# Odd residues' odd wavenumbers as pairs of 64-row products, and the filter's odd rows loaded between w2's tiles

## The chip, the cores and the metric

The kernel runs on one NeuronCore of one Trainium2 chip. The metric is device time in microseconds (us) of one execution. Three runs of the kernel before took 126.07, 126.17 and 126.58 us; their median is 126.17.

## The reference

Two branches work on sequences of S = 2048 rows, and a gate mixes them.

```python
def _A_ref(x, w_r, w_i):
    X = rfft2(x, axes=(-2, -1)); X = X * (w_r + 1j * w_i)
    return irfft2(X, s=(S, D), axes=(-2, -1))
def _B_ref(x, w1, b1, w2, b2):
    h = layernorm(x)
    u = gelu(einsum("bsd,sf->bdf", h, w1) + b1)
    return (einsum("bdf,fs->bds", u, w2) + b2).transpose(0, 2, 1)
g = sigmoid((x * gate_w).sum(-1)); out = g * a + (1 - g) * b
```

x is 2048 x 512 in bf16, w_r and w_i are 2048 x 257, w1 is 2048 x 1792 and w2 is 1792 x 2048. Branch A is a two-dimensional Fourier transform, a multiplication by a complex filter and the inverse transform; branch B is a layer norm and two dense layers that mix the rows.

## The kernel before, in words

**Dense layers.** The first layer (`m1`, L716) is 14 tiles of F by 16 row tiles j, 224 matmuls of 128x512; its weights sit in one buffer `wa` (tiles 0 to 6) and two buffers `wb` (7 to 10 and 11 to 13). Its results go through a gelu (L732). The second (`m2`, L1065) is again 14 by 16 matmuls. w2's tiles use the same buffers again: tile group 0 can be loaded only when the last L716 on `wa` is over, the last three tiles only when L716 is over altogether. Six PSUM banks (four `acc`, in places two `fb`) hold sums of `m2` that are not finished.

**Transform.** Rows are split by residue r modulo 4. The forward transform along rows is done with table products (L565 to L568) and a radix-4 butterfly on VectorE (`radix4`), then along columns (L664). Wavenumbers along the rows are kept in two halves: `lt` = 0 the even ones, `lt` = 1 the odd ones. `tb2` builds the array B of each half with a few edge columns (L686 to L688). The filter sits in `W` and is multiplied in by two products for each half (`mul`, L839), `comb` and `ob`. Mean and Nyquist columns are treated apart in `c0a`, `c0b`, `c0c`, the Nyquist row in `nyq` on a single partition (L810 to L815); a small path `lines`, `linem` repairs row 0 of B through two small DMAs and a matmul.

The inverse transform along the rows (`i1`, `i1s`) makes, for each half h of the columns and each residue r, a product of B with a table `ti`. For odd residues the even wavenumbers go through `i1s` (L897): the rows are cut in two halves of 64, each half is a product of its own, into a bank of its own (fa, fb), and VectorE adds and subtracts the two (`eo2`, L905). The odd wavenumbers of odd residues go through `i1` with 128 rows and 256 columns (L925), and ScalarE copies the result straight to `zz` (L940). Then `fq`, the inverse transform along the columns (`i3`, L1008 to L1012), the scaling by the gate (L1016), and the sum with branch B (L1071, L1078, L1084).

**Order.** All work is given to a planner as tasks: engine, duration, what is read and written, and a priority. It simulates the engines by its own durations and writes down one order for each engine; that order is fixed in the program, and an engine waits where an input is not there. Lower numbers of `prio` go first: transform products have 0 to 5, `m1` 10, `m2` 20, so dense matmuls fill the places where no transform product is ready. All loads but three are issued by SyncE (SP) in one queue order.

**Filter loads.** `ld_W` (L435) loads one component (real, imaginary) with 16 DMAs: four for `wt` (two of them single rows), whose rows PE turns round with a flip matrix (`wf`, L768, copied by L772 and L780), eight for the odd wavenumbers' rows, three for the even ones (one a single row) and one for the Nyquist row `wn`. `wprep` (L789) needs both components.

## Time and profile before

| what | value |
|---|---|
| median of three runs | 126.17 us |
| profiled execution | 126.11 us |
| its span (first to last instruction) | 124.3 us |
| PE busy | 119.8 us, 96% of the span |
| VectorE (DVE) busy | 113.2 us, 91% |
| ScalarE (ACT) busy | 83.7 us, 67% |
| DMA traffic | 23.10 MB |
| granted PE clock | full in all slices |

Busy time of PE is the union of the matmuls' spans; matmuls are pipelined and their ends are modelled, so the distance from start to start tells what one costs. L numbers are lines of the kernel before. In the order of time, the first column is the start in us from the span's start, the second the time in us, then engine, line, operation, output<-input with shapes, a count, and in brackets the idle time before it and who ended it. In a list of waits the numbers are: us in total, times, longest us.

### The profile page before, as it was taken

Reading aid. Unit: us, or ns where it says so; the run is one execution under the profiler, and the core shown is the slowest. Engines: PE = TensorE matmul, PEld = TensorE weight load, DVE = VectorE, ACT = ScalarE, POOL = GpSimd, SP = SyncE. Lnnn points to the kernel's source line nnn. Section 1 sums busy time; section 2 is a strip of 40 time slices with the busy share of each in tenths; the row PEclk is TensorE's granted clock in tenths of the full one; section 3 lists DMA queues with packets and bytes.
Section 4 is the critical chain, followed back from the end, with each engine's and each line's share of the span. In section 5 each row is a group of like instructions: output and inputs, shape, how many; then the busy total and the mean of one; then the engine's idle time right before and its main releaser. Section 6 shows DMA issues by size and latency. Waiting matters only on the chain.

```text
span 124.3 us, 2226 instructions
## 1 busy us (share of the span) xinstructions
PE 119.8 (96%) x789; PEld 67.7 (54%) x789; DVE 113.2 (91%) x271; ACT 83.7 (67%) x176; POOL 0.2 (0%) x4
## 2 busy tenths in 40 slices
PE   7799999999999999999999999999999999999990
PEld 2245555555645466644445555555577576665590
DVE  1789999999999999999999999999969999999951
ACT  3696889699999999999520003742279999993200
POOL 0000000000000000000000000000000000000000
PEclk9999999999999999999999999999999999999999
DMA  3999999992459946699999930000000000003751
GB/s 112 316 329 306 397 394 385 376 300 62 112 121 258 289 97 121 157 395 406 420 414 415 422 132 0 0 5 0 3 0 0 5 0 0 0 12 131 287 211 42
DMA packets 18203, 23.10 MB, mean 186 GB/s; under 512 B 2174, under 2 KB 15888, under 8 KB 18192
## 3 DMA queue, kind: packets, MB, share of 16 engines
q1 hardware_dynamic: 17616, 22.34, 52.9%
q10 hardware_dynamic: 576, 0.62, 1.6%
q8 instruction: 6, 0.10, 0.3%
q14 instruction: 5, 0.04, 0.1%
HBM read 20.84 MB, written 2.10 MB: 185 GB/s over the span
## 4 chain that ended last, share of the span: by engine, by line
PE 93%; DMA 2%; DVE 1%; ACT 0%; issue 0%
PE acc L1065 33%; PE acc L716 31%; PE fb L716 6%; PE fb L1065 6%; PE fa L716 3%; DMA x<-in_A_x_dram 2%; PE fb L664 1%; PE fa L664 1%; PE fa L565 1%; PE fa L566 1%; PE fa L897 1%; PE fb L1012 1%; PE fa L1012 1%; PE fa L568 1%; PE fa L567 1%; PE fb L925 1%
## 5 line engine op out<-in xcount | busy, mean ns | idle before, releaser
L716 PE MATMUL acc<-h,wb 128*128 128x512 bf16 x112 | 27.0, 379 | 0.0
L1065 PE MATMUL acc<-gl,wb 128*128 128x512 bf16 (+1 forms) x98 | 24.7, 372 | 0.0
L1065 PE MATMUL acc<-gl,wa 128*128 128x512 bf16 (+1 forms) x98 | 24.0, 371 | 0.0
L1071 ACT ACTIVATE x<-acc,ombb,omg 128x512 bf16<-128x512 f32 x12 | 9.0, 780 | 19.3 <-PE acc L1065 19.3
L1065 PEld LDWEIGHTS <-wa 128*128 128x128 bf16 x126 | 13.4, 113 | 9.6
L1065 PEld LDWEIGHTS <-wb 128*128 128x128 bf16 x126 | 13.2, 114 | 9.4
L716 PE MATMUL acc<-h,wa 128*128 128x512 bf16 x64 | 17.1, 379 | 0.0
L716 PEld LDWEIGHTS <-wb 128*128 128x128 bf16 x112 | 10.7, 98 | 10.3
L716 PEld LDWEIGHTS <-wa 128*128 128x128 bf16 x112 | 10.3, 98 | 10.9 <-DMA wa<-in_B_w_dram 1.1
L489 DVE BATCH_NORM_STATS2 stats<-x 128x6 f32<-128x512 bf16 x12 | 8.1, 676 | 2.1 <-DMA x<-in_A_x_dram 2.1
L746 ACT ACTIVATE x<-x 128x512 bf16<-128x512 bf16 x16 | 10.0, 654 | 0.0
L571 ACT CAST xp<-fa 128x512 bf16<-128x512 f32 x16 | 9.0, 594 | 1.5 <-PE fa L568 1.4
L716 PE MATMUL fb<-h,wa 128*128 128x512 bf16 x32 | 9.9, 379 | 0.0
L732 ACT ACTIVATE gl<-acc,b1f 128x512 bf16<-128x512 f32 x11 | 7.8, 711 | 2.8 <-PE acc L716 2.8
L537 ACT ACTIVATE h<-x,nmr,rstd 128x512 bf16<-128x512 bf16 x11 | 8.4, 806 | 1.3 <-DVE nmr L528 1.1
L716 PE MATMUL fa<-h,wa 128*128 128x512 bf16 x16 | 6.1, 378 | 0.9 <-DVE h L531 0.9
L664 PEld LDWEIGHTS <-X 128*128 128x128 bf16 x64 | 4.7, 98 | 2.2
L1016 ACT ACTIVATE B<-fb,g 128x512 bf16<-128x512 f32 x8 | 5.5, 689 | 0.0
L1016 ACT ACTIVATE B<-fa,g 128x512 bf16<-128x512 f32 x8 | 5.5, 685 | 0.0
L671 ACT CAST X<-fb 128x512 bf16<-128x512 f32 x8 | 5.1, 639 | 0.0
L671 ACT CAST X<-fa 128x512 bf16<-128x512 f32 x8 | 5.1, 635 | 0.0
L741 DVE TENSOR_TENSOR x<-x,gw 128x2048 bf16<-128x2048 bf16 x4 | 4.7, 1214 | 0.0
(183 smaller groups left out, 234.8 us busy)
## 6 DMA issues: line engine op xcount, KB each, us to landing
wb<-in_B_w_dram SPq DMA_DIRECT2D x11, 512.0 KB
wa<-in_B_w_dram SPq DMA_DIRECT2D x7, 512.0 KB
wa<-in_B_w_dram SPq DMA_DIRECT2D x2, 896.0 KB
wb<-in_B_w_dram SPq DMA_DIRECT2D x4, 384.0 KB
out_dram<-x SPq DMA_DIRECT2D x3, 512.0 KB
x<-in_A_x_dram SPq DMA_DIRECT2D x2, 512.0 KB
wa<-in_B_w_dram SPq DMA_DIRECT2D x4, 224.0 KB
rot<-dft_ti SPq DMA_DIRECT2D x1, 768.0 KB
```

Source lines behind the costliest of these rows:

```text
L489: V.bn_stats(out=t["stats"][:, j, :], in_=t["x"][:, j // 4, j % 4, :])
L537: add("ACT", 0.71, lambda j=j: A.activation(t["h"][:, j // 4, j % 4, :], t["x"][:, j // 4, j % 4, :], ActF.Identity, bias=t["nmr"][:, j:j ...
L571: add("ACT", act(512), lambda r=r, dq=dq: A.copy(xe(r)[:, :, :, dq, :], t["pa", r, dq][:]), reads=[("pa", r, dq)], writes=[("X", r, dq)], ...
L664: T.matmul(pb[:, k % 2, k // 2], lhsT=t["X"][:, lt, EX[e], c, k, :], rhs=tbl(k, c), start=True, stop=True)
L671: A.copy(t["X"][:, lt, EX[e]].rearrange("p c j l -> p (c j l)").rearrange("p (h c g b) -> p h c g b", h=2, c=2, b=2)[:, :, c], t["pb", lt, ...
L716: T.matmul(t["u", ft][:], lhsT=w[:, j // 4, j % 4, c * P:(c + 1) * P], rhs=t["h"][:, j // 4, j % 4, :], start=(j == jorder[0]), stop=(j == ...
L732: gelus.append(add("ACT", act(512, 1) , lambda ft=ft: A.activation(t["gl"][:, ft, :], t["u", ft][:], ActF.Gelu_apprx_tanh, bias=t["b1f"][: ...
L741: add("DVE", tt(2048), lambda r=r: V.tensor_mul(t["x"][:, :, r, :], t["x"][:, :, r, :], t["gw"][:, None, :].to_broadcast([P, 4, D])), read ...
L746: A.activation(t["x"][:, q, r, :], t["x"][:, q, r, :], ActF.Copy, accum_out=t["glog"][:, 4 * q + r:4 * q + r + 1])
L1016: A.activation(eo_v(p)[:, n].rearrange("p h (n w) -> p h n w", w=2), t["i3", j][:].rearrange("p h (w n) -> p h n w", w=2), ActF.Copy, scal ...
L1065: T.matmul(t["y", j, m][:, cs], lhsT=w[:, o, 512 * q + r:512 * q + 512:4], rhs=t["gl"][:, ft, cs], start=(ft == 0), stop=(ft == NFT - 1))
L1071: A.activation(tbuf(j).rearrange("p h d -> p (h d)"), t["y", j, 0][:], ActF.Identity, bias=t["ombb2"][:, j:j + 1], scale=t["omg"][:, j:j + 1])
```

## The change

The odd wavenumbers of odd residues are now made as the even ones are: `i1s` runs for both halves `lt`, with 64-row products in pairs, one into an fa and one into an fb bank. For this the odd wavenumbers are stored in another order (`sig`, blocks of 16 rows), so that the partners of a pair lie 64 rows apart; the table `ti` shrinks from 3072 to 2112 columns. For `lt` = 1, `eo2` makes the sum, the difference, and from the difference's two parts a sum and a difference again; a factor of the square root of 2 that is left out there goes into the even half's table (`root`) and out again through the gate `g` (`omga`). As before ScalarE copies two banks for each group, now into `zo`.

The loads of the filter follow the new row order. `ld_W` keeps the four large DMAs of even rows; the single rows go into tasks of their own (`single`); the odd rows come in 16 tasks of two DMAs with 64 rows each (`ld_odd`), whose priorities lie between those of w2's tiles. w1's last four loads move between the two components of `ld_W`.

Several small VectorE operations change too: `sp0` and two operations of `sp1` go; the edge columns of `tb2` take fewer operations, and two of them move to ScalarE (`tb2c`); `c0a` and the first part of `omg` move to ScalarE; `c0b` is done once for both halves; `wprep` now waits for the second `bfly`; the Nyquist row is spread over 16 partitions by a DMA (`nspread`), and `nyq` comes after the first half's `ob`; the flips `wf` wait for gelu 7 and 9; `linem` comes after the second `ob`.

```diff
     p = np.arange(P)
-    r4 = np.arange(4)
+    sig = 97 - 32 * (p % 64 // 16) + 2 * (p % 16) - p // 64
...
-    ti = np.zeros((P, 3072))
+    ti = np.zeros((P, 2112))
...
-        th = ang(s, 1 + 4 * (p ^ 96), S)
+        th = ang(s, 1 + 4 * sig, S)
...
+            root = np.where(p < 64, 1.0, 2.0 ** 0.5)
+            v[:, 0:P], v[:, P:256] = np.cos(th), -np.sin(th)
+            v[0, P:256] = alt * (0.5 ** 0.5 if r == 1 else -(0.5 ** 0.5))
+            v[:, 0:P] *= root
+            v[:, P:256] *= root
+            th = ang(1 + 4 * sig, s[0:64], S)
+            v[:, 256:320], v[:, 320:384], v[:, 384:448] = -np.sin(th), np.cos(th), np.sin(th)
...
-        t["wn"] = sb([1, 2, WL], BF16, "wn")
+        t["wn"] = sb([16, 2, 17], BF16, "wn")
+        t["vs"] = sb([16, 2, 16], BF16, "vs")
+        t["na"] = sb([16, 2, 2, 16], F32, "na")
+        t["nn"] = sb([16, 2, 16], BF16, "nn")
         t["ta"] = sb([P, 4, 640], BF16, "rot")
...
-            add("SP", 0.5, ld_wb(k, q), writes=[("w1", k + 1, 4 * q + r) for r in range(4)], prio=10 + 12 * k + 0.1 * q,
+            add("SP", 0.5, ld_wb(k, q), writes=[("w1", k + 1, 4 * q + r) for r in range(4)], prio=(17.1 + q // 2 + 0.2 * (q % 2)) if k else 10 + 0.1 * q,
...
+            dma(t["wn"][:, comp, 0:16], wsrc[comp][1024, 0:256].rearrange("(a b) -> a b", b=16))
...
+        w, u, v, z = rows(comp)
+        dma(u[64:127], v[65:128, :, 0])
+        dma(u[0:64], v[64:128, :, 2])
+        dma(w[1:64, 0, :, 0], v[1:64, :, 0])
+        dma(w[64:P, 0, :, 0], v[0:64, :, 2])
+
+    def ld_odd(comp, n):
+        w, u, v, z = rows(comp)
+        h, o = n % 2, n // 2
+        dma(w[64 * h:64 * h + 64, 1, o, 1], v[:, 3 - o, 3].rearrange("(o i h) l -> h o i l", o=4, h=2)[h][:, ::-1])
+        c, f = 64 * h + 16 * o, 97 - 32 * o - h
+        dma(w[c:c + 16, 1, :, 0], v[f:f + 31:2, :, 1])
 
     for comp in range(2):
-        add("SP", 12.3, ld_W(comp), writes=[("W", comp), ("wt", comp)], prio=17 + 8 * comp, nbytes=300000, after=[a0])
-        if comp == 0:
-            load_wb(1)
+        add("SP", 2.1, lambda comp=comp: ld_W(comp), writes=[("W", comp), ("wt", comp)], prio=17 + comp, nbytes=530000, after=[a0], late=(3.0, 4.0)[comp])
+        for n, at in enumerate((0.2, 0.25, 0.4, 15.8, 15.9)[:5 - comp]):
+            add("SP", 0.6, lambda comp=comp, n=n: single(comp, n), writes=[("Ws", comp, n)], prio=17 + comp + at, nbytes=2000, after=[a0], late=1.0)
+    load_wb(1)
+    for k in range(16):
+        add("SP", 1.0, lambda k=k: ld_odd(k // 8, k % 8), writes=[("Wl", k // 8, k % 8)], prio=31.25 + 0.5 * (k * 7 // 12) + 0.01 * k if k < 12 else 36 + 0.01 * k, nbytes=190000, after=[a0], late=0.5)
...
-    add("DVE", tiny(1), sp0, reads=dk, writes=["sp"], prio=0)
...
-        V.tensor_scalar_mul(sd[:, 0, 0, 1], sd[:, 1, 1, 1], c)
-        V.tensor_scalar_mul(sd[:, 1, 0, 1], sd[:, 0, 1, 1], -c)
-        V.tensor_add(fx[:, 1, 0], sp[:, 0, 1], sd[:, 0, 0, 1])
-        V.tensor_sub(fx[:, 3, 0], sp[:, 0, 1], sd[:, 0, 0, 1])
-        V.tensor_sub(fx[:, 1, 1], sd[:, 1, 0, 1], sp[:, 2, 1])
-        V.tensor_add(fx[:, 3, 1], sd[:, 1, 0, 1], sp[:, 2, 1])
-    add("DVE", tiny(12), sp1, reads=["sp"], writes=["fx"], prio=0)
+        for i, k in ((1, c), (3, -c)):
+            V.scalar_tensor_tensor(fx[:, i, 0], sd[:, 1, 1, 1], k, sp[:, 0, 1], op0=Alu.mult, op1=Alu.add)
+        for i, f in ((1, Alu.subtract), (3, Alu.add)):
+            V.scalar_tensor_tensor(fx[:, i, 1], sd[:, 0, 1, 1], -c, sp[:, 2, 1], op0=Alu.mult, op1=f)
+    add("DVE", tiny(10), sp1, reads=dk, writes=["fx"], prio=0)
...
-                        for i in range(2):
-                            bh, vh = b[:, i::2], v[:, 2 * i:2 * i + 2]
-                            V.tensor_sub(bh[:, :, 1:3, 0], vh[:, :, 0, 0:4:3, 0], vh[:, :, 1, 0:4:3, 0])
-                            V.tensor_copy(bh[:, :, 0:4:3, P], vh[:, :, 0, 1:3, 0])
-                            V.tensor_copy(bh[:, :, 1:3, P], vh[:, :, 1, 1:3, 0])
+                        V.tensor_sub(*tb2e(lt, 1, 0), tb2v(lt)[:, :, :, 1, 0:4:3, 0])
+                        if lt == 0:
+                            for k in (0, 2):
+                                V.tensor_copy(*tb2e(lt, k, P))
...
+    def tb2c():
+        for k in (0, 2):
+            A.copy(*tb2e(1, k, P))
+    add("ACT", 0.45, tb2c, reads=[("R", 1, i, c) for i in range(4) for c in range(2)], writes=[("B", 1, i) for i in range(4)], prio=4.4)
...
-        V.tensor_scalar(t["omg"][:], t["g"][:], -0.5, 0.5, op0=Alu.mult, op1=Alu.add)
-        V.tensor_scalar(t["g"][:], t["g"][:], 0.5, 0.5, op0=Alu.mult, op1=Alu.add)
...
-    add("DVE", 0.4, omg, reads=["b2h"], writes=["g", "omg"], prio=0)
...
+    def omga():
+        A.activation(t["omg"][:], t["g"][:], ActF.Copy, bias=0.5, scale=-0.5)
+        A.activation(t["g"][:], t["g"][:], ActF.Copy, bias=0.5, scale=0.5)
+        A.activation(t["g"][64:P, 1:NJ:2], t["g"][64:P, 1:NJ:2], ActF.Copy, scale=0.5 ** 0.5)
+    add("ACT", 0.6, omga, reads=[], writes=["g", "omg"], prio=4.5)
+    add("DVE", 0.15, omg, reads=["b2h"], writes=["g", "omg"], prio=0)
...
-                add("PE", mm(256, 256), wf, reads=[("wt", comp), "flip"], writes=[("pw", comp, lt, a)], prio=5, alloc=[tag])
+                add("PE", mm(256, 256), wf, reads=[("wt", comp), ("Ws", comp, 0), ("Ws", comp, 1), "flip"], writes=[("pw", comp, lt, a)], prio=5, alloc=[tag], after=[gelus[7 + 2 * comp]])
...
-    add("DVE", 0.4, wprep, reads=[], writes=[("W", 0), ("W", 1), "wpm"] + wtk, prio=1)
+    wpt = add("DVE", 0.2, wprep, reads=[("W", 0), ("W", 1)] + wtk + [("Wl", comp, n) for comp in range(2) for n in range(8)], writes=["wpm"], prio=1)
...
-        def c0a(lt=lt):
-            b, c0 = t["B"][:, lt], t["c0"][:, lt]
...
-        add("DVE", 0.2, c0a, reads=bk, writes=[("c0", lt)], prio=0)
...
+            def c0a():
+                b, c0 = t["B"], t["c0"]
+                A.copy(c0[:, :, :, 0, :], b[:, :, :, 0:2, 0])
+                A.copy(c0[:, :, :, 1, :], b[:, :, :, 3:1:-1, 0])
+            add("ACT", 0.45, c0a, reads=[("B", i, e) for i in range(2) for e in range(4)], writes=[("c0", i) for i in range(2)], prio=4.5)
+        if lt == 0:
+            def nspread():
+                for v in range(2):
+                    dma(t["vs"][:, v], t["B"][0:1, 0, 0, 2 + v, :].rearrange("p (a b) -> p a b", b=16))
+            b0 = [("B", 0, e) for e in range(4)]
+            add("SP", 1.0, nspread, reads=b0, writes=["vs"], prio=34.45, nbytes=1024, late=1.0)
...
             def nyq():
-                pz = sb([1, 1280], F32, "X")
-                na = pz[:, 0:1024].rearrange("p (i v l) -> p i v l", i=2, v=2)
...
-                    V.tensor_mul(na[:, i], v, wn[:, i, None, 0:L].to_broadcast([1, 2, L]))
...
+                V.tensor_mul(na[:], t["vs"][:, None].to_broadcast([16, 2, 2, 16]), wn[:, :, None, 0:16].to_broadcast([16, 2, 2, 16]))
...
-            add("DVE", 3 * d1(512) + 0.35, nyq, reads=[("B", i, e) for i in range(2) for e in range(4)] + [("W", 0), ("W", 1), ("c0", 0)] + pbk, writes=["nn"], prio=0.5)
...
-        def c0b(lt=lt):
...
+            nyt = add("DVE", tiny(6), nyq, reads=["vs", ("Ws", 0, 3), ("Ws", 0, 4), ("Ws", 1, 3), ("c0", 0)], writes=["nn"], prio=3.25)
...
+        def c0b():
...
+            V.tensor_mul(cm[:, 0], c0[:, :, :, 0], pm[:, 0])
...
+        if lt == 0:
+            add("DVE", tiny(6), c0b, reads=[("c0", 0), ("c0", 1), "wpm"], writes=[("ce", 0), ("ce", 1)], prio=3.22)
...
-        add("DVE", 2 * tt(2048), bfly, reads=bk, writes=["xs"], prio=pr)
+        bt = add("DVE", 2 * tt(2048), bfly, reads=bk, writes=["xs"], prio=pr)
+        if lt:
+            wpt.deps.add(bt)
...
-            add("DVE", tt(4096), mul, reads=["xs", ("W", comp), ("W~", comp, lt)], writes=[("pp", "st")[comp]], prio=pr)
+            add("DVE", tt(4096), mul, reads=["xs"] + ([("Wl", comp, n) for n in range(8)] if lt else [("W", comp), ("W~", comp, 0)] + [("Ws", comp, n) for n in range(3)]), writes=[("pp", "st")[comp]], prio=pr)
...
+        obt = add("DVE", tt(2048) + 2 * tt(1024), ob, reads=["xs"], writes=bk, prio=pr)
+        if lt == 0:
+            nyt.deps.add(obt)
...
-                dma(t["s9"][8:9], t["nn"].rearrange("p v l -> p (v l)"))
+                for v in range(2):
+                    dma(t["s9"][8:9, L * v:L * v + L].rearrange("p (a b) -> p a b", b=16), t["nn"][:, v])
...
-    add("PE", mm(512), linem, reads=["s9", "tb"], writes=["pl8"], prio=3, alloc=["fa"], after=[combt])
+    add("PE", mm(512), linem, reads=["s9", "tb"], writes=["pl8"], prio=3, alloc=["fa"], after=[obt])
...
-        if rs:
-            def i1s(h=h):
...
+        for lt in range(2 * rs):
+            def i1s(h=h, lt=lt):
...
+                p2 = t["i1s", h, lt] = [ps([P, 2, 2, P], F32, tag, 2) for tag in ("fa", "fb")]
...
+                            f = (320 - 64 * c) if lt else c * P
...
-                                T.matmul(p2[m][:, n, v], lhsT=t["B"][k, 0, r, 2 * c + v, h:L:2], rhs=ti[k, 2 * c * P:2 * c * P + P], start=(c == 0), stop=(c == 1))
-            i1t[h, 1, 0] = i1t[h, 3, 0] = add("PE", MMR, i1s, reads=[("T", 0, 1), "ti"], writes=[("i1s", h)], prio=3, alloc=["fa", "fb"])
+                                T.matmul(p2[m][:, n, v], lhsT=t["B"][k, lt, r, 2 * c + v, h:L:2], rhs=ti[k, f:f + P], start=(c == 0), stop=(c == 1))
...
+            def eo2(h=h, lt=lt):
+                e, o = (t["zo"][:, lt, h, m ^ lt] for m in range(2))
+                if lt == 0:
+                    for k, f in enumerate((V.tensor_add, V.tensor_sub)):
+                        f(t["zz"][:, 1, h, 0, :, k].rearrange("p v r a -> p r v a"), e, o)
+                    return
+                zv = t["zz"][:, 1, h, 1].rearrange("p v k r a -> p r (v k) a")
+                x = lambda u: u.rearrange("p r v (k a) -> p r (v k) a", k=2)
+                V.tensor_add(zv[:, :, :, 0:64], x(e), x(o))
+                V.tensor_sub(e, e, o)
+                V.tensor_sub(zv[:, :, 0:4:2, 64:P], x(e)[:, :, 0:4:2], x(e)[:, :, 1:4:2])
+                V.tensor_add(zv[:, :, 1:4:2, 64:P], x(e)[:, :, 0:4:2], x(e)[:, :, 1:4:2])
+            add("DVE", 2 * tt(512) + 2 * tt(256) * lt, eo2, reads=[("zo", h, lt, m) for m in range(2)], writes=[("zz", h, r, lt) for r in (1, 3)], prio=3.55)
...
-            for lt in range(rs, 2):
-                tag = ("fa", "fb")[lt if not rs else r // 2]
+            for lt in range(0 if rs else 2):
+                tag = ("fa", "fb")[lt]
...
-                        if r % 2:
-                            for c in range(2):
-                                f = (5 - c) * P
-                                T.matmul(p1[:, v], lhsT=d(c), rhs=ti[:, f:f + L], start=(c == 0), stop=(c == 1))
...
-                        V.tensor_copy(k0[:, :, :, 0], e[:, :, :, 0])
-                        V.tensor_copy(k1[:, :, :, 0], e[:, :, :, P])
+                        V.tensor_copy(t["zz"][:, 0, h, :, :, :, 0, 0].rearrange("p i v k -> p (i v) k"), e[:, :, :, 0:P + 1:P].rearrange("p i v k -> p (i v) k"))
```

More of the change, by code (lines that the diff above doesn't have):

```diff
@@ L460, in ld_ti @@
     def ld_ti():
-        t["ti"] = sb([P, 3072], BF16, "rot")
+        t["ti"] = sb([P, 2112], BF16, "rot")
         dma(t["ti"][:], tabs["ti"])
@@ L948 @@
+                add("ACT", act(512), i1ev, reads=[("i1", h, r, lt)] + pbk, writes=[("ze", h, r, lt)], prio=1.7, free=[tag], after=[lined])
             if r % 2 == 0:
```

153 lines of the change are left out of this document (64 added, 89 removed).

## The prediction

> **What bounds the kernel now.** I read the page first, sections 1, 2 and 4: TensorE (PE) is busy in every slice but the first two and the last, and the chain that ended last is nearly all matmul.
>
> ```profile
> span 124.3 us, 2226 instructions
> ...
> PE 119.8 (96%) x789; PEld 67.7 (54%) x789; DVE 113.2 (91%) x271; ACT 83.7 (67%) x176; POOL 0.2 (0%) x4
> ...
> PE   7799999999999999999999999999999999999990
> ...
> DVE  1789999999999999999999999999969999999951
> ...
> PE 93%; DMA 2%; DVE 1%; ACT 0%; issue 0%
> ```
>
> Busy need not mean useful, so the waits come next, PE's alone and then the list of all engines.
>
> ```profile
> PE fa L716 <- DVE h L531: 0.9, 1, 0.9
> PE fa L361 <- PEq L1117: 0.8, 1, 0.8
> ```
>
> Both lie before 5.3 us. From there to 121.5 us PE waits for nobody: wherever the transform is not ready, matmuls of the two dense layers (L716, L1065) stand in the order. So a part of PE's work that becomes shorter shortens the end by as much, as long as nobody keeps PE waiting.
>
> VectorE (DVE) is nearly as full, so I looked at the end of its order of time for slack.
>
> ```profile
> 117.49 0.68 DVE L1084 TENSOR_TENSOR x<-x,B 128x1024 bf16<-128x1024 bf16 x1
> 118.41 0.75 DVE L1078 SCALAR_TENSOR_TENSOR x<-acc,omg,x 128x512 bf16<-128x512 f32 x1 [0.23 <-PE acc L1065]
> 119.94 0.48 DVE L1078 SCALAR_TENSOR_TENSOR x<-acc,omg,x 128x256 bf16<-128x256 f32 x1 [0.78 <-PE acc L1065]
> 120.72 0.35 DVE L1078 SCALAR_TENSOR_TENSOR x<-fa,omg,x 128x128 bf16<-128x128 f32 x1 [0.30 <-PE fa L1065]
> 121.50 0.35 DVE L1078 SCALAR_TENSOR_TENSOR x<-fb,omg,x 128x128 bf16<-128x128 f32 x1 [0.43 <-PE fb L1065]
> ```
>
> It waits for PE 0.23 + 0.78 + 0.30 + 0.43 = 1.74 us here: DVE may come about 1.7 us later before the last store moves.
>
> **PE: the products that are replaced.** The old and the new form both stand in PE's order of time, for the old L925 is what goes and the old L897 is what the new ones copy.
>
> ```profile
> 93.73 0.60 PE L925 MATMUL fa<-rot,B 128*128 128x256 bf16 x4
> 94.17 0.22 PE L933 MATMUL fb<-rot,B 128*128 128x128 bf16 x1
> ...
> 96.14 0.59 PE L1065 MATMUL acc<-gl,wb 128*128 128x512 bf16 x2
> 96.66 0.23 PE L897 MATMUL fa<-rot,B 64*128 64x128 bf16 x1
> 96.67 0.23 PE L897 MATMUL fb<-rot,B 64*128 64x128 bf16 x1
> ...
> 97.22 0.62 PE L1065 MATMUL acc<-gl,wb 128*128 128x512 bf16 x2
> 97.77 0.23 PE L897 MATMUL fa<-rot,B 64*128 64x128 bf16 x1
> ...
> 98.33 0.84 PE L1065 MATMUL acc<-gl,wb 128*128 128x512 bf16 x3
> ```
>
> Ends are modelled, so I count from start to start. Four L925 take 94.17 - 93.73 = 0.44 us; there are 16, so 1.75 us go. A group of 16 L897 (8 pairs, the two halves of a pair 0.01 us apart) lies between dense matmuls, which step 0.216 us: the two that start at 96.14 would be over at 96.57, the next starts at 97.22, so the group costs 0.65; the second, from 97.65 to 98.33, 0.68. Of that 8 x 0.055 = 0.44 are the pairs; the remaining 0.22 is paid on going from 128-row to 64-row products and back. Two such groups come in: 1.33 us. Gain 1.75 - 1.33 = 0.42 us. The bounds: nothing if the new groups cost double (no row shows that), and 1.75 - 2 x 0.44 = 0.87 if each new group lies directly beside an old one, so that the change of form is shared. I take 0.42, because a group needs one fa and one fb bank at once, and the copies out of them (ScalarE, ACT, L900) come 0.48 us apart, 0.98 to 1.1 us per group:
>
> ```profile
> 97.32 0.60 ACT L900 CAST h<-fa 128x512 bf16<-128x512 f32 x1
> 97.80 0.61 ACT L900 CAST h<-fb 128x512 bf16<-128x512 f32 x1
> 98.43 0.58 ACT L900 CAST h<-fa 128x512 bf16<-128x512 f32 x1
> ```
>
> So two dense matmuls (0.43 us) fit between groups, as now. The Trainium skill, TensorEngine Tiling (Array Packing), says under Theoretical Speedup that a contraction of at most 64 rows gains up to twofold, and under Key Properties that a change of tiling mode drains the engine; by the first the gain would be 0.87, by the second less, and this trace shows the second with its 0.22 us.
>
> **DVE: what goes.** From start to start: L621 and two of L634 to L639, 0.42; the twelve edge operations of L686 to L688 become four, eight at 0.07, 0.57; L800 and L801 twice, to ACT, 0.29; the one-row Nyquist line L810 to L815, from 58.36 to 60.79, 2.43; L820 to L825 twice, 1.01; L789 and L790 0.20; two of L752 to L754 0.27. Before the first filter multiply (L839, 61.15 us) 5.19 us leave. Some of it comes back later: the Nyquist line on 16 rows (six tiny ones, 0.08 each, 0.5), L820 to L825 once (0.5), L789 and L790 (0.2). So DVE stands 4.0 us earlier at the inverse transform. There the paired form asks for more: in place of a plain copy by ACT, eo2 for the odd wavenumbers adds, per half, two 512-element operations (L905 steps 0.34 to 0.37) and two of 256 elements; the nearest rows are L1038 with 129 (0.22) and L955 with 508 (0.34), and I take 0.20 to 0.34, low end. That is 1.08 per half, 2.16 in all, at most 2.7. Two L953 copies become one in each half, -0.15. Net 5.19 - 1.20 + 0.15 - 2.16: DVE ends its own work 2.0 us earlier (1.4 at the high end). It is not the bound, so this is worth nothing by itself; it is cover.
>
> **ACT.** Seven tiny operations arrive (edges, c0, g); the nearest row, L1025 with 128x8, steps 0.11, so 0.8 us. ACT is full from 30 to 57 us and then waits 12.3 us for L1065, in which they are hidden. Copies out of PSUM stay at 16. Cover gone, they would delay copies by 0.8 us.
>
> **SP and the DMAs.** The filter comes in 32 DMAs now (24.44 to 50.47 us, w1's last four between), and w2's first tile is issued at 50.70, though its buffer is free at 35, when L716 turns from wa to wb. After: 8 large, 9 small, 32 of 64 rows, and three more for the Nyquist line, 20 more. A filter DMA takes SP 0.43 (at 33.04) to 0.67 (at 34.61), so +9 to 13 us of issuing. The even rows and w1 should be out by 36 to 43 us, w2's seven tiles (now 3.33 us) and 24 odd pieces (10 to 16, nearer 11, since most of the odd pieces now take 0.43 to 0.52) by 51 to 57, the rest by 62. Waiting behind them are w2's tiles 7 to 10, now issued at 54.14. First use is at 63.7, and with tiles 0 to 6 alone six banks give 42 dense matmuls, 9 us, so PE is covered to 72.8. The last three tiles wait for PE at 63.75 in both kernels. The odd rows are read by DVE at about 67.5. Cost 0; cover about 5 us for DVE. The added waits: filter flips L768 stand behind a gelu, queued before the dense matmuls; the last ACT copies of them end at 55.2 now, DVE would come to the multiply at 56.0. The one-row DMA to 16 rows stands on SP ahead of w2's tile 7, which waits for its buffer then anyhow.
>
> **The sum.** The profiled execution took 126.11 us, its span 124.3 with 1.8 around it, 0.06 below the median 126.17. 126.11 - 0.42 = 125.69, say 125.7. Start and tail (5.3 us and 2.9 us) are untouched.
>
> **Rivals.**
> (A) As forecast, gain 0.2 to 0.6: 125.5 to 125.9. 55%.
> (B) Groups side by side: 0.62 with one such pair, 0.87 with two, 125.2 to 125.5. For it: DVE is 4 us earlier, so all inputs are there when the odd part begins; against it: the two banks. 16%. The twofold gain of the Trainium skill, TensorEngine Tiling (Array Packing), Theoretical Speedup, would lead here.
> (C) The gain is eaten: groups meet more 128-row products between them, or PE's order, which is fixed beforehand from planned times, has small waits: 126.0 to 126.6. For it: every task's planned time changes. Against it: the present order, from the same planner, has no wait. 13%.
> (D) Slower: the filter's rows become the bound. If DVE's 5.19 us are lost at the multiply (flips or odd rows late), DVE ends 1.20 - 0.15 + 2.16 = 3.2 us later than now; 1.74 - 0.42 = 1.3 of that is hidden, so 1.9 us come on top of 125.69: 127.6. It decides from about 3.7 us of waiting at the filter multiplies. Against it: the flips' copies end at 55.2 already now. 9%.
> (E) Slower: PE itself stands before a transform product or a w2 tile, because real landings fall behind the planned ones; 1 us gives 126.7, 2 us 127.7. 7%.
>
> **Numbers.** 0.5% is about what a measurement of this kernel can tell from no change, 0.63 us: faster is below 125.54, slower above 126.80. Faster: B and a tenth of A, 0.22. Slower: D, E and a fifth of C, 0.19. Same: the rest, 0.59. The range that leaves out no more than 2 in 10 is 125.2 to 126.9. A's own is 125.5 to 125.9.
>
> **What would show it.** The 128x256 products at L925 are gone and 64 matmuls of 64x128 stand there, pairs 0.055 us apart; dense matmuls lie between the groups and start 0.65 to 0.68 us apart around each. PE still waits for nothing after 5.3 us. DVE's first filter multiply starts at 56 and its waits for PE at the end grow to more than 3 us. w2's first tile is issued between 36 and 43 us. I am wrong if PE has a wait over 0.3 us on DVE, ACT or a DMA, or if the new groups cost more than 0.87 us each.

## The result and the profile after

The changed kernel takes 132.76 us (median of six runs, 131.60 to 134.51), against 126.12 us of the kernel before in the same runs. The ratio is 1.0507, with a 95% interval from 1.0456 to 1.0557: slower by 5%. The forecast was 125.7 us, between 125.2 and 126.9. The profiled execution took 132.86 us. Below, a median counts all runs of a kernel, while a ratio leaves out those more than 1.5% above the kernel's fastest, so the two can differ.

From the page of the changed kernel: span, busy time, the slices of PE and of its clock, and the chain by engine.

```profile
span 131.1 us, 2256 instructions
...
PE 121.6 (93%) x791; PEld 66.9 (51%) x805; DVE 112.1 (86%) x253; ACT 85.7 (65%) x183; POOL 0.2 (0%) x4
...
PE   7799999999999999999916999999999999999991
...
PEclk9999999999999999999995599999999999999999
...
PE 68%; DVE 10%; DMA 8%; ACT 8%; SPq 2%; issue 2%; DVEq 0%
```

One place stands out: PE is busy for a tenth of the 21st slice (65.6 to 68.8 us) and for six tenths of the 22nd, and its clock is half in the 22nd and 23rd. The chain, 93% PE before, has only 68% PE now and runs in parts through DMAs and SP's queue (SPq). The list of waits (us in total, times, longest us) names w2's tiles and the filter's imaginary rows:

```profile
PEld L1102 <- DMA wb<-in_B_w_dram: 5.8, 4, 2.8
DVE wpm L813 <- DMA W<-in_A_w_i_dram: 4.3, 1, 4.3
PE acc L1102 <- DMA wb<-in_B_w_dram: 4.1, 3, 2.5
```

L1102 is the second dense layer (L1065 before), L813 the part of `wprep` that reads the filter's imaginary component. PE's order of time around the empty slices:

```profile
63.74 1.67 PE L1102 MATMUL acc<-gl,wa 128*128 128x512 bf16 x7
65.25 0.38 PE L1102 MATMUL acc<-gl,wb 128*128 128x512 bf16 x1
66.51 0.41 PE L1102 MATMUL acc<-gl,wb 128*128 128x512 bf16 x1 [0.88 <-DMA wb<-in_B_w_dram]
69.39 0.62 PE L1102 MATMUL acc<-gl,wb 128*128 128x512 bf16 x1 [2.48 <-DMA wb<-in_B_w_dram]
69.80 0.63 PE L1102 MATMUL acc<-gl,wa 128*128 128x512 bf16 x1
71.15 0.62 PE L1102 MATMUL acc<-gl,wb 128*128 128x512 bf16 x1 [0.72 <-DMA wb<-in_B_w_dram]
71.56 2.77 PE L1102 MATMUL acc<-gl,wa 128*128 128x512 bf16 x6
```

After only seven matmuls on w2's tiles 0 to 6 (`wa`), the order asks for tile 7 (`wb`, at 65.25), which landed at 65.17, and then for tiles 8, 9 and 10, which land at 66.46, 69.35 and 71.11. A dense matmul at full clock steps 0.216 us. From start to start the three waits are 1.26 - 0.22 = 1.04, 2.89 - 0.22 = 2.67 and 1.35 - 0.43 = 0.92 us, together 4.63. From 69.39 on the matmuls step 0.427 us (six from 71.56 take 74.12 - 71.56 = 2.56 us), that is at half clock, until 75.1; against 0.216 this costs 2.35 us more. 4.63 + 2.35 = 6.98; less the 0.38 us that the products gain (below) it is 6.60, and PE's last matmul ends 6.80 us later than before (128.26 against 121.46). The other 0.2 us is not assigned; part of it is the start, where the first dense matmul stands 0.05 us later.

SP's order of time shows when the tiles went out:

```profile
40.03 0.37 SPq L307 DMA_DIRECT2D wa<-in_B_w_dram  x1
40.46 2.48 SPq L307 DMA_DIRECT2D W<-in_A_w_r_dram  x4
...
56.13 2.54 SPq L307 DMA_DIRECT2D W<-in_A_w_i_dram  x4
58.72 0.45 SPq L307 DMA_DIRECT2D wa<-in_B_w_dram  x1
59.22 1.04 SPq L307 DMA_DIRECT2D W<-in_A_w_i_dram  x2
60.37 1.26 SPq L307 DMA_DIRECT2D vs<-B  x2
61.72 1.95 SPq L307 DMA_DIRECT2D wb<-in_B_w_dram  x4
63.72 7.72 SPq L307 DMA_DIRECT2D W<-in_A_w_i_dram  x8
...
72.49 1.32 SPq L307 DMA_DIRECT2D wb<-in_B_w_dram  x3
```

A task of two odd-row DMAs keeps SP for 1.04 to 1.27 us, so between two of w2's first seven tiles lie 2.6 to 4.5 us; tile 6 goes out at 58.72 and tiles 7 to 10 from 61.72, 7.6 us later than before (54.14). The last three tiles stand behind the last eight odd-row DMAs and go out at 72.49, 8.7 us later than before. Up to 61 us SP's issuing sets this pace, and not the transfers; this is seen in the busy times by stretch (columns: stretch, its length, busy PE, PEld, DVE, ACT and POOL with their instructions, granted clock, DMA engines' share, GB/s). The kernel before:

```profile
56.00:61.00 5.00, 5.00 (x25) 2.29 (x24) 4.86 (x33) 4.88 (x15) 0.00 (x0) 1.00 1.02 410
```

The changed kernel in the same stretch:

```profile
56.00:61.00 5.00, 4.95 (x24) 2.29 (x24) 4.96 (x5) 4.75 (x17) 0.00 (x0) 1.00 0.66 202
```

Before, seven w2 tiles were queued at once and the DMA engines were full at 410 GB/s. After, they are busy for two thirds and move half as much, while SP is issuing in all but about 0.9 us of the five. Behind 64 us this turns round: from 65 to 69 us the engines are full (share 0.98, 347 GB/s; the row stands in the last section), and tiles 9 and 10 take 6.6 and 7.9 us from issue to landing, where tile 7 took 3.45.

What was to be gained did come in its place. The new pairs, in PE's order of time:

```profile
97.03 0.81 PE L1102 MATMUL acc<-gl,wa 128*128 128x512 bf16 x3
97.77 0.23 PE L939 MATMUL fa<-rot,B 64*128 64x128 bf16 x1
97.78 0.23 PE L939 MATMUL fb<-rot,B 64*128 64x128 bf16 x1
...
98.33 0.84 PE L1102 MATMUL acc<-gl,wa 128*128 128x512 bf16 x3
```

A group lies between 97.03 + 3 x 0.216 = 97.68 and 98.33, 0.65 us, the lower end of what was predicted. DVE's first filter multiply (L868) starts where it was expected, and the second half waits:

```profile
56.16 2.28 DVE L868 TENSOR_TENSOR xp<-xp,W 128x4096 bf16<-128x4096 bf16 x1
...
73.01 0.19 DVE L813 TENSOR_TENSOR wpm<-W 128x16 f32<-128x16 bf16 x1 [4.30 <-DMA W<-in_A_w_i_dram]
...
125.20 0.75 DVE L1115 SCALAR_TENSOR_TENSOR x<-acc,omg,x 128x512 bf16<-128x512 f32 x1 [1.26 <-PE acc L1102]
```

At the end DVE still waits 1.26 + 0.78 + 0.30 + 0.43 = 2.8 us for PE, so its 4.3 us of waiting are hidden behind PE's own loss.

### The profile page after: what moved, and what is told of

Same layout as the page of the kernel before. It is cut to its first block, busy times and chain, and to the rows that moved or that the text cites. A ratio compares the mean times of both kernels' runs of the same rounds, so it can differ in the third digit from the quotient of the medians.

```text
span 131.1 us, 2256 instructions
## 1 busy us (share of the span) xinstructions
PE 121.6 (93%) x791; PEld 66.9 (51%) x805; DVE 112.1 (86%) x253; ACT 85.7 (65%) x183; POOL 0.2 (0%) x4
## 4 chain that ended last, share of the span: by engine, by line
PE 68%; DVE 10%; DMA 8%; ACT 8%; SPq 2%; issue 2%; DVEq 0%
PE acc L1102 31%; PE acc L735 13%; DMA wb<-in_B_w_dram 6%; PE fb L735 5%; PE fb L1102 5%; ACT X L677 3%; PE fa L735 3%; ACT x L765 3%; DMA x<-in_A_x_dram 2%; SPq L307 2%; DVE st L868 2%; DVE xp L868 2%; PE fa L939 2%; DVE B L695 2%; PE fa L576 1%
## 5 line engine op out<-in xcount | busy, mean ns | idle before, releaser
L1102 PE MATMUL acc<-gl,wb 128*128 128x512 bf16 (+1 forms) x94 | 25.0, 383 | 4.5 <-DMA wb<-in_B_w_dram 4.1
L735 PE MATMUL acc<-h,wb 128*128 128x512 bf16 x108 | 26.3, 379 | 0.1
L1102 PE MATMUL acc<-gl,wa 128*128 128x512 bf16 (+1 forms) x96 | 25.1, 390 | 0.1
L1102 PEld LDWEIGHTS <-wb 128*128 128x128 bf16 x126 | 13.3, 115 | 15.4 <-DMA wb<-in_B_w_dram 5.8
L1102 PEld LDWEIGHTS <-wa 128*128 128x128 bf16 x126 | 13.5, 115 | 10.6 <-issue 1.4
L735 PE MATMUL acc<-h,wa 128*128 128x512 bf16 x62 | 16.6, 379 | 0.1
L735 PEld LDWEIGHTS <-wa 128*128 128x128 bf16 x112 | 10.3, 98 | 10.9 <-DMA wa<-in_B_w_dram 1.5
L1121 DVE TENSOR_TENSOR x<-x,B 128x1024 bf16<-128x1024 bf16 x7 | 4.8, 683 | 0.0
```

What stands on the lines that cost most here:

```text
L735: T.matmul(t["u", ft][:], lhsT=w[:, j // 4, j % 4, c * P:(c + 1) * P], rhs=t["h"][:, j // 4, j % 4, :], start=(j == jorder[0]), stop=(j == ...
L1102: T.matmul(t["y", j, m][:, cs], lhsT=w[:, o, 512 * q + r:512 * q + 512:4], rhs=t["gl"][:, ft, cs], start=(ft == 0), stop=(ft == NFT - 1))
L1121: V.tensor_add(o, o, eo_v(p))
```

## The experiments

**Theory 1:** the loads cost all of it. SP's queue cannot issue 32 small DMAs among w2's tiles in the time that the planner assumes, so PE's order, written for planned landings, stands before tiles that have not landed. The plan itself says that tiles 7 to 10 have landed at 61.4, 62.8, 64.1 and 65.5 us; tiles 8 to 10 really landed 3.7, 5.3 and 5.7 us later. Not all of this begins between w2's tiles: tile 7 goes out 6.75 us later than planned, and the first w2 tile already goes out 4.7 us late (40.03, planned 35.31), ahead of the first odd-row DMA. **Theory 2:** the transfers are too slow whoever issues them. **Theory 3:** the new products, edges or DVE's order cost something too.

**The odd rows issued by GpSimd.** The 32 DMAs leave SP's queue.

```diff
-        dma(w[c:c + 16, 1, :, 0], v[f:f + 31:2, :, 1])
...
+        dma(w[c:c + 16, 1, :, 0], v[f:f + 31:2, :, 1], nc.gpsimd)
...
+        add("POOL", 1.0, lambda k=k: ld_odd(k // 8, k % 8), writes=[("Wl", k // 8, k % 8)], prio=31.25 + 0.5 * (k * 7 // 12) + 0.01 * k if k < 12 else 36 + 0.01 * k, nbytes=190000, after=[a0], late=0.5)
```

> The changed kernel with one edit: the 32 DMAs of the filter's odd rows are issued by GpSimd's queue instead of SyncE's; w2's tiles stay on SyncE. Theory 1 (SyncE's queue: the odd pieces take 0.45 to 1 us each of its time, so w2's tiles 7 to 10 are issued at 61.7 and 11 to 13 at 72.5, PE waits 4.6 us and then runs at half clock, 2.4 us more): w2's last three tiles are issued at about 63.8, PE waits for no tile, 125.5 to 126.0. Theory 2 (the packets of 514 bytes between the tiles slow the tiles in the DMA engines, whoever issues them): PE still waits over 2 us for w2, 129 or more. Theory 3 (the 64-row products or VectorE's chain cost the time): 132 as now.

131.86 us, ratio 1.041 (1.034 to 1.048). The waits behind 57 us were gone, but a new loss took their place. GpSimd, which had nothing else to do, began at 1.27 us, while x and w1 were being loaded. Busy times in the same stretch, first of the kernel before:

```profile
5.00:30.00 25.00, 24.71 (x140) 12.84 (x141) 23.45 (x71) 20.81 (x45) 0.00 (x0) 1.00 0.99 334
```

Then of this run:

```profile
5.00:30.00 25.00, 20.94 (x120) 10.54 (x120) 20.60 (x61) 18.28 (x40) 14.92 (x26) 1.00 1.09 275
```

PE lost 3.8 us there; the DMA engines were full in both, but moved 275 GB/s instead of 334. So this run took away one loss and added another, and could not tell the theories apart.

**The even rows issued by GpSimd,** with the same edit on `ld_W` and `single`.

> The changed kernel with one edit: the filter's even rows and single rows (8 large and 9 small DMAs) go to GpSimd's queue; the odd pieces still alternate with w2's tiles on SyncE. Theory 1: SyncE begins the alternating part some 8 to 10 us earlier (40.0 now), so all is issued in time: PE waits less than 1 us, 125.5 to 127. Theory 2: the alternation with small packets is unchanged, so the tiles stay slow; they only begin earlier, PE still waits for the tiles issued after 61 us, 128 or more. Theory 3: 132.

139.63 us, ratio 1.096 (1.087 to 1.106). The same start, worse: PE was busy for 16.69 us of that stretch, and, with the odd pieces still on SP, PE waited for tiles at 74.5 to 78.4 us all the same.

**The loads alone, on the kernel before.** Its products, edges and tables stay; the filter is loaded with the change's tasks, priorities and 64-row pieces (in the old row order).

```diff
+        dma(w[64 * h:64 * h + 64, 1, o, 1], v[:, 3 - o, 3].rearrange("(o i) l -> o i l", o=4)[2 * h:2 * h + 2, ::-1])
+        c, f = 32 * o + 16 * h, 96 - 32 * o + 16 * h
+        dma(w[c:c + 16, 1, :, 0], v[f:f + 16, :, 1])
```

> The kernel before with the changed kernel's loads alone: odd rows in 32 DMAs of 64 rows between w2's tiles, same priorities, the filter preparation after the second butterfly as there; PE's products, the row order and the small VectorE operations are those of before. Theory 1 and 2 (the loads are the cause): PE waits 3 to 6 us for w2's tiles between 64 and 76 us and its clock falls, 131 to 134. Theory 3 (products or VectorE): 126 to 126.6.

The profiled execution took 328 us, and the other three 131.18 to 134.88 us, which gives no ratio. In this profile the clock is not on record, and its matmuls of 512 columns step 0.48 or 0.62 us, so the half clock that the next expectation speaks of is not shown.

> The same kernel as the one before with split loads, for a profile: three of its four executions took 131 to 135 us, and the profiled one 328 with PE at half clock throughout. Theory 1: 131 to 135, PE waits 3 to 6 us for w2's tiles between 64 and 76 us. Otherwise the loads alone don't explain it: 126 to 127.

134.82 us, ratio 1.064 (1.058 to 1.071). Its list of waits has the loss of the changed kernel:

```profile
PEld L1079 <- DMA wb<-in_B_w_dram: 5.8, 6, 2.5
PE acc L1079 <- DMA wb<-in_B_w_dram: 4.0, 3, 2.1
...
PE fa L780 <- DMA wt<-in_A_w_i_dram: 1.6, 1, 1.6
```

So the loads, without any of the new products, are enough for the whole 5%. That it is more comes in part from the last row: here the flips (L780) wait 1.6 us for their even rows, which they don't in the changed kernel. Theory 3 isn't needed for the loss.

**The same DMAs, other numbers for the planner.** Only what the planner believes of a task of odd rows is changed, so the fixed orders come out differently; what is transferred and by whom stays. PE's order changes most, SP's a little (here `ti`'s table goes out behind the last three tiles). Three versions; the first:

```diff
-        add("SP", 1.0, lambda k=k: ld_odd(k // 8, k % 8), writes=[("Wl", k // 8, k % 8)], prio=31.25 + 0.5 * (k * 7 // 12) + 0.01 * k if k < 12 else 36 + 0.01 * k, nbytes=190000, after=[a0], late=0.5)
+        add("SP", 1.3, lambda k=k: ld_odd(k // 8, k % 8), writes=[("Wl", k // 8, k % 8)], prio=31.25 + 0.5 * (k * 7 // 12) + 0.01 * k if k < 12 else 36 + 0.01 * k, nbytes=450000, after=[a0], late=2.5)
```

> The changed kernel with one edit in the planner's numbers: a task of two odd pieces counts 1.3 us of SyncE (1.0 before), 450 kB (190 kB) and lands 2.5 us late (0.5). The DMAs and their priorities stay. Theory 1a (the tiles are late, but what hurts is that PE's order was written for earlier landings: it has tile 7's product second in line when other products are possible): PE's waits shrink to under 1.5 us, 126 to 128.5. Theory 1b (the tiles are so late that no order helps): 131 to 133.

127.77 us, ratio 1.0106 (1.0071 to 1.0141), with 126.53 us before: over 5 of the 6.6 us are back. PE has no wait behind 5.9 us and full clock until 123.9, though tiles 7 to 10 go out from 60.09, only 1.6 us earlier than in the changed kernel, and the last three at 69.39. Now the plan is too late: transform products stand further back than they need to, and DVE waits for them. From the list of waits:

```profile
DVE X L991 <- ACT h L983: 5.2, 1, 5.2
```

The nearer numbers (1.3 us, 380000 bytes, 0.5 us):

> As the run with true durations, but less pessimistic: an odd task counts 1.3 us, 380 kB and lands 0.5 us late, so that the plan's last odd rows (69.2 to 70.5 us) and w2's last tile (76.3) lie nearer to what the trace of that run shows (issued until 69.3 and at 70.7), and the inverse transform's first product is planned at 86.3 and not at 90.4. There the plan was 4 us too late for VectorE, which stood 5.2 us before the inverse transform and then ended last. Theory 1a (the loss is the distance between the planned and the real landings, on either side): PE waits under 0.7 us, VectorE's wait before the inverse transform falls to 1 to 2 us, 125.5 to 126.5. Rival (the loads, late as they are, cost over 1 us under any order): 127 to 129.

127.0 us (125.86 to 128.9, twelve runs; before, 126.24), ratio 1.0024 (0.9992 to 1.0056). In the profiled execution (127.94 us) PE stood some 1.65 us before w2's tiles between 65 and 71 us, and DVE waited 1.9 us, in the old places. From the list of waits:

```profile
PEld L1102 <- DMA wb<-in_B_w_dram: 2.9, 4, 1.2
...
DVE wpm L813 <- DMA W<-in_A_w_i_dram: 1.9, 1, 1.9
```

Expected were 125.5 to 126.5 us and waits of PE under 0.7. The runs of this version lie 3 us apart. It may be that each execution's landings show in its time where the order leaves no room; only one was profiled, so this is not shown. Between the two versions (410000 bytes, 1.5 us):

> Only the planner's numbers for a task of odd rows: 1.3 us, 410000 bytes, 1.5 us late, between the two versions that gave 127.77 (planned too late, PE idle at the end) and 127.0 (planned a little early, PE waits 1.65 us at 65 to 71). Theory 1 (the distance between planned and real landings is the loss): PE's waits for w2 at 65 to 71 fall under 0.8 us while DVE's wait for ACT in the inverse transform stays under 2 us; 126.0 to 126.7. Rival (any order pays, since the transfers themselves are too slow): what PE gains at 65 to 71 is lost at DVE, 127.0 to 127.7.

127.18 us, ratio 1.0047 (1.0014 to 1.0081), with PE's waits for w2 at 1.6 us in the profiled execution, counted as before. It was neither better than the nearer numbers nor as free of waits as the later ones; the sizes that theory 1 gave here did not come out. With all 32 DMAs on SP, none of the three sets of numbers left both PE and DVE free of these waits in the profiled execution. By the ratio the nearer numbers may cost nothing (its interval includes 1); by the medians they cost 0.6%.

**Half as many odd-row DMAs.** The loads alone on the kernel before, alternating as in the change, but 16 DMAs with 128 rows.

> The kernel before with the loads split and alternating as in the run before, but each odd DMA with 128 rows, as the kernel before has them: 16 in place of 32. Alternation and priorities stay, the number is halved, the planner counts 0.5 us for each. Theory 1 (it is SyncE's time for 32 pieces): SyncE is through 6 to 8 us earlier, w2's last tiles go out at 64 to 66 us, PE waits under 1 us, 126 to 127.5. Rival (the alternation itself, whatever the number): PE waits 3 us or more, 130 or more.

128.01 us, ratio 1.0103 (1.0047 to 1.0158). The list of PE's waits in its profile:

```profile
PE fa L781 <- DMA wt<-in_A_w_i_dram: 1.9, 1, 1.9
PE fa L729 <- DVE h L544: 0.9, 1, 0.9
```

No wait for w2 is left: tiles 7 to 10 went out from 57.24 and landed at 62.0 to 66.3, 3.2 to 3.5 us earlier than with 32 DMAs in the run before (65.5 to 69.4). The wait alone would not show it, because PE comes to w2 3.7 us later here: it stands at 38 us, where the flips (L781) wait for their even rows (in the change they stand behind a gelu), and its clock is half from 41.0 to 44.5. A PE 3.7 us earlier would have waited about 0.4 us for tile 10, by an estimate from these landings. So 16 DMAs that alternate make the tiles less late than 32 do, and most of PE's wait goes with them. The expected 126 to 127.5 us, with the last tiles out by 64 to 66, were missed: they went out at 67.60.

**The odd rows on GpSimd, not at the start.** A copy on GpSimd that reads `b2h` stands ahead of them.

> The odd rows on GpSimd's queue again, but its first DMA stands behind a copy of two elements of b2h, which lands at about 26 to 30 us. In the run without that hold GpSimd began at 1.3 us and took DMA time from x and w1 (PE waited 4 to 5 us before 30 us), while after 57 us PE waited for nothing. Theory 1 (SyncE's queue is what made w2 late): PE waits for nothing over 0.3 us after 5.3 us, w2's last tiles are issued at about 64 us, 125.4 to 126.0. Theory 2 (odd packets slow w2's or w1's tiles wherever they are issued): PE waits for a tile between 30 and 75 us, 127 or more.

129.15 us (126.55 to 133.59, twelve runs), ratio 1.0098 (1.0049 to 1.0148). `b2h` landed only at 34 us, so 32 DMAs ran into w2's loads. The profile is of the execution with 133.59 us. SP issued tiles 7 to 10 from 56.94 on, and yet PE had to wait for them until 67.6 to 70.5; here too the plan had them 4.3 to 5.1 us earlier than they landed. Its busy times by stretch:

```profile
56.00:61.00 5.00, 5.00 (x25) 2.25 (x24) 4.97 (x5) 4.75 (x18) 2.13 (x5) 1.00 1.07 261
61.00:65.00 4.00, 4.00 (x21) 1.86 (x19) 4.00 (x6) 2.49 (x8) 1.90 (x4) 1.00 1.03 305
```

Here the DMA engines are full (share 1.07, 1.03) and move 261 to 305 GB/s instead of 410. In the run with the odd rows on GpSimd from the start it was 275 instead of 334. So theory 2 holds in this form: while GpSimd issues small pieces, the full engines move less of the large tiles. For the changed kernel it does not explain why the tiles go out late, as its engines stood at 0.66 there; but from 65 to 69 us, when tiles 8 to 10 are under way, they are full as well, and what part of those landings this makes no run separates.

**Only some of the pieces on GpSimd,** with the nearer numbers: the last four pieces, or the last eight, behind a GpSimd copy that reads a gelu's result.

```diff
+        nc.gpsimd.tensor_copy(t["pj"][:], t["gl"][0:1, 9, 0:2])
+    add("POOL", 0.3, hold, reads=[("gl", 9)], writes=["pj"], prio=0)
+    for k in range(12, 16):
+        add("POOL", 1.2, lambda k=k: ld_odd(k // 8, k % 8, nc.gpsimd), writes=[("Wl", k // 8, k % 8)], prio=1 + 0.01 * k, nbytes=190000, after=[pl.last_w["pj"]], late=1.5)
```

> The changed kernel with the nearer durations (1.3 us and 380000 bytes for a task of odd rows), and the last four pieces (8 DMAs of the imaginary component) issued by GpSimd behind a copy that waits for the tenth gelu, so at about 54 us, instead of by SP before w2's last three tiles. Theory 1 (SP's queue is what holds w2 back): SP is rid of the 7 us that those 8 take behind tiles 7 to 10, the last three tiles go out at 64 to 66 instead of 71.8, PE waits under 0.5 us at 65 to 71, and the time is 125.7 to 126.2. Theory 2 (the 16 DMA engines are the limit, whoever issues): the landings of tiles 7 to 10 do not come earlier, PE waits 1.5 us or more as with nearer durations alone, 126.8 to 127.5.

126.37 us (126.17 to 127.08, twelve runs), ratio 1.0005 (0.9987 to 1.0024); expected were 125.7 to 126.2. SP's order of time in its profile:

```profile
63.05 1.95 SPq L307 DMA_DIRECT2D wb<-in_B_w_dram  x4
65.04 0.46 SPq L307 DMA_DIRECT2D rot<-dft_ti  x1
65.60 1.93 SPq L307 DMA_DIRECT2D wb<-in_B_w_dram  x3
```

And the list of PE's waits, which is complete:

```profile
PE fa L358 <- PEq L1161: 0.8, 1, 0.8
PE fa L735 <- DVE h L542: 0.4, 1, 0.4
```

PE's order of time where it comes to w2:

```profile
63.72 4.05 PE L1109 MATMUL acc<-gl,wa 128*128 128x512 bf16 x18
67.61 0.59 PE L1109 MATMUL acc<-gl,wb 128*128 128x512 bf16 x2
```

Tiles 7 to 10 go out even later than in the changed kernel (61.72) and land later (66.67 to 71.44), and PE waits for none of them: by the plan of this version tile 7 lands at 67.1 us, so the order has 18 matmuls on tiles 0 to 6 first. Two things changed at once here. The planner's numbers move this order; the four pieces on GpSimd do not make tiles 7 to 10 land earlier than with the nearer numbers alone (66.07 to 71.35), but they take away most of the 7 us of SP ahead of the last three tiles (out at 65.60, not 71.79), and DVE's wait of 1.9 us is gone. The whole 5% is back with the same products and the same odd rows.

> As the run with four pieces on GpSimd, but eight, all of the imaginary component (16 DMAs), behind the ninth gelu, so from about 49 us. Theory 1: tiles 7 to 10 go out at 54 to 57 as in the kernel before, PE has no wait behind 5.9 us, 125.6 to 126.0. Theory 2: w2's tiles 3 to 8 share the DMA engines with GpSimd's pieces and land late though issued early; PE waits 1 to 4 us at 60 to 71, 126.8 to 130.

126.44 us, ratio 1.0013 (0.9994 to 1.0031). No wait for a tile either. Tiles 7 to 10 went out from 59.90, not at 54 to 57 (by the plan 57.7 was the earliest), and GpSimd began at 44.38, not at 49; the expected time of 125.6 to 126.0 was not reached.

**Everything but the loads.** The changed kernel's products, DVE and ACT work and table, with the loads of the kernel before. It leaves out the new row order of the odd rows.

> All of the change but its loads: products, DVE, ACT and table ti are the changed kernel's; the filter comes in with the DMAs and in the places of the kernel before (16 for a component, all before w2's first tile; only the Nyquist row goes to 16 partitions). So the odd rows stand in the old order and the output is wrong in the odd wavenumbers; the amounts of work are the changed kernel's. Theory 1 (the loads cost everything, the products are worth what their distances say): PE has no wait after 5.9 us and the time is 126.1 - 0.42 = 125.7, with 125.4 to 125.9. Rival (part of the loss sits in products, edges or the order of DVE, and has been hidden behind the loads): 126.5 or more, with waits of PE on DVE or ACT behind 60 us.

126.01 us (125.91 to 127.05, twelve runs) against 126.2, ratio 0.9993 (0.997 to 1.0016); expected were 125.4 to 125.9. The list of PE's waits has nothing behind 5.5 us:

```profile
PE fa L358 <- PEq L1158: 0.8, 1, 0.8
PE fa L739 <- DVE h L546: 0.2, 1, 0.2
```

Summed from start to start, the 48 old products of the odd residues (L925 and L897) took 1.75 + 1.11 = 2.85 us before; here the 64 pairs' halves take 2.22. The dense matmuls of 512 columns took 45.56 us and now take 45.81, which is the switch into two more groups. Net gain 0.38 us. The last matmul ends at 121.37 instead of 121.46, only 0.09 us earlier: the start and the first layer took 0.28 us more (the first dense matmul stands at 5.42 instead of 5.29, as x's first rows were there 0.14 us later, and there is one wait of 0.14 us at 22.6). Theory 3 falls: without the new loads, the change costs nothing that these runs can tell, and its gain is too small to be told from no change. Tiles 7 to 10 land at 65.96 to 69.82 here, later than with the kernel before, and PE waits for none, as the plan has them at 65.5 to 69.6.

## Why the prediction was wrong

**The step that failed** is "SP and the DMAs", with its result "Cost 0". Its single parts:

- The first w2 tile "between 36 and 43": 40.03, right. "w2's seven tiles and 24 odd pieces by 51 to 57": 60.3. The rate per DMA was right: 24 odd ones kept SP for 11.9 us ("nearer 11") and w2's seven tiles for 3.8 (3.3). What stood nowhere are 1.1 us for three DMAs of the Nyquist row and 3.4 us in which SP issued nothing, together 20.2 us from 40.03 on. The last eight odd pieces took 7.72 us: 4.3 of issuing and 3.4 of waiting. In this trace SP's DMAs take eight semaphores in turn, and none goes out before the one eight places ahead of it has landed: the last two odd pieces go out at 69.36 and 71.12, as tiles 9 and 10 land (69.35, 71.11). SP's waits in the changed kernel:

```profile
SPq L307 <- DMA wa<-in_B_w_dram: 5.4, 6, 1.7
...
SPq L307 <- DMA wb<-in_B_w_dram: 4.0, 5, 1.9
```

- "The rest by 62": the last odd piece was out by 71.4, and with it "the last three tiles wait for PE at 63.75 in both kernels". In the changed kernel they wait for SP until 72.49. This cost PE nothing more here, as PE was late by then.
- "PE is covered to 72.8 by 42 dense matmuls of tiles 0 to 6". This is the error that cost the time. Six banks and seven tiles would allow 42; the order that PE follows has seven of them, and then asks for tile 7. I worked out what PE could do, not what its fixed order does. The run with the last four pieces on GpSimd uses that freedom: 18 matmuls on `wa` before the first on `wb`, and no wait, with landings that are later than the changed kernel's.
- "Cover about 5 us" for the odd rows at DVE: DVE needed them at 68.7 and had them at 73.0. That would have been rival D, hidden here behind PE.

The landings of tiles 7 to 10 side by side (planned: by the kernel's own planner; waits: PE's for these tiles, from start to start):

| kernel | go out from | planned to land | landed | first matmul on tile 7 | PE waits |
|---|---|---|---|---|---|
| before | 54.14 | 65.5 to 69.6 | 64.48 to 68.17 | 65.93 | none |
| changed | 61.72 | 61.4 to 65.5 | 65.17 to 71.11 | 65.25 | 4.63 us |
| nearer numbers | 62.65 | 64.7 to 68.8 | 66.07 to 71.35 | 66.11 | 1.65 us |
| later numbers (first version) | 60.09 | 66.0 to 70.0 | 63.56 to 68.96 | 66.96 | none |
| last four on GpSimd | 63.05 | 67.1 to 71.2 | 66.67 to 71.44 | 67.61 | none |
| products alone | 57.34 | 65.5 to 69.6 | 65.96 to 69.82 | 66.22 | none |

The tiles went out 7.6 to 6.4 us later than before, but landed only 0.7 to 2.9 us later: before, tile 7 stood behind the first seven tiles and took 10.3 us from issue to landing, here 3.45. What moved more is the plan, 4.1 us earlier than before, so that PE's order asked for tiles 8 to 10 before they were there.

**Rival E is what happened:** PE stands before a w2 tile because real landings fall behind the planned ones. It was named with 7% and priced at 126.7 for 1 us and 127.7 for 2 us. Two sizes were missing from it: the wait was 4.6 us, and a further 2.35 us came from the half clock behind it, a term that stood nowhere. With its own rule (125.7 plus the wait) 4.6 us give 130.3, and 132.7 with the half clock, which is the measured time.

**Right were the other steps.** The new groups cost 0.65 us each; the gain on PE is 0.38 where 0.42 was written, though only 0.19 of it is seen between the medians, and the interval includes no gain. Rival B did not occur: there is a dense matmul or more between any two groups. DVE's first multiply started at 56.16 (56.0 predicted). In the run with the products alone DVE ends its own work at 117.07 instead of 118.17, 1.1 us earlier instead of 1.4 to 2.0, of which 0.47 us is a wait for the Nyquist row's DMA that the account had not got. ACT's 0.8 us did not reach PE: with the products alone it has no wait on ACT. The prediction's own test, "I am wrong if PE has a wait over 0.3 us on a DMA", pointed to the right place.

## What to carry to other kernels

Where an engine's order is fixed from planned times, compare these planned landings with real ones before counting on work that could fill a wait; the same transfers cost 6.6 us with one plan and 0.8 to 1.2 us with others. When many small DMAs are put into one queue among large ones, add up that queue's issue times piece by piece to the issue of each large tile, with its waits for DMAs that are still under way; then ask whether the tile lands later too, since here a tile that went out 7.6 us later landed 0.7 us later. And a wait of a few microseconds on PE can have a second price behind it, in matmuls at half clock.

## What the runs showed of the hardware

**Half clock behind waits.** Tile 7's matmul was over at 65.47, and until 69.39 PE had one more, at 66.51. The matmuls from 69.39 on step 0.427 instead of 0.216 us. The granted clock on record fell at 68.27, 2.8 us after tile 7's matmul and 1.5 us into the longest wait. The stretch in the changed kernel (the last three columns are granted clock, DMA share and GB/s):

```profile
65.00:69.00 4.00, 1.03 (x4) 0.23 (x2) 3.60 (x10) 0.00 (x0) 0.00 (x0) 0.91 0.98 347
69.00:73.00 4.00, 2.89 (x7) 0.88 (x8) 0.00 (x0) 0.00 (x0) 0.00 (x0) 0.50 0.35 81
```

Full clock came back at 75.10, 3.95 us after the last wait. The Trainium skill, TensorE: Matmul & The Clock Gate (Part 1: The HAM clock gate), gives at least one idle window of about 3.4 us ahead of half rate and about 3.4 us of sustained work ahead of full rate. The trace roughly agrees with the second, with 3.95 us. It does not agree with the first: one matmul stood inside the 2.8 us, and no single wait was over 2.7 us. The length of one wait does not decide it either. In the loads alone with 128 rows half clock began 1.15 us after a wait of 1.9 us, in the loads alone with 64 rows a wait of 2.1 us had none behind it, and with nearer numbers waits of up to 1.1 us had none. Half clock lasted 6.83 us in the changed kernel and 3.42 us in both runs with the loads alone. What decides it is not shown.

**Small DMAs.** An odd-row DMA has 32 KB and keeps SP for 0.5 us (mean of 32; 0.32 to 0.76), and a w2 tile has 512 KB and keeps it for 0.35 to 0.53 us (one took 1.34). So the small ones fill SP's time with a sixteenth of the bytes, and the engines were busy for 0.66 of 56 to 61 us. By the Trainium skill, DMA: Bandwidth & Descriptors (Bandwidth, Measured), transfers under 64 KB are dominated by descriptors. The 202 GB/s of that stretch don't show this, as the engines were idle for a third of it; what is nearer to it is that full engines moved 261 to 305 GB/s while GpSimd's 32 KB pieces were among the tiles, instead of 410.

**GpSimd as a second queue.** It takes the issue off SP, but its pieces share the DMA engines with what SP has under way: full engines moved 261 to 305 GB/s instead of 410. The run with 8 of the 32 DMAs there, from 49 us, took 126.37 us, and the run with all of them, from 35.75 us, 129.15. The two also differ in the planner's numbers, so what the number of pieces is worth alone was not separated.

**Left open.** In the profiles of kernels with the new products x's first rows reach DVE between 3.40 and 3.95 us, in four of kernels with the old ones between 3.14 and 3.41. PE's first dense matmul stands up to 0.6 us later there, which is more than the whole gain; the cause stays open.
